# A gated memory-attention mixer and MLP on one core: two side units fewer in the third step, x requested ahead of weights, the last full output pass ahead of the last side units

## The chip, the core and the metric

The kernel runs on one core of a Trainium2 chip. The metric is the device time of one execution in microseconds (us). Engines are TensorE (PE, with its weight loads PEld), VectorE (DVE), ScalarE (ACT), GpSimd (POOL) and SyncE (SP), which here only issues DMAs. A line number such as L689 is a line of the kernel as it was before; where the changed kernel is meant, lines from L587 on stand two lower in the file (L689 is L691 there; those between L901 and L903 one lower).

## What is computed

Two branches over the same 2048 tokens of 512 channels, mixed by a gate per token. Branch A is an attention of 32 heads of 128 that goes through the tokens in 64 segments of 32, one after the other, since the first 8 rows of each segment's output are the memory of the next. Branch B is a layer norm and an MLP of width 1376.

```python
for s in range(n_seg):                       # 64 segments, a recurrence through mem
    xs = x[:, s * seg_len:(s + 1) * seg_len, :]
    h = jnp.concatenate([mem, xs], axis=1)   # 8 + 32 rows
    q = jnp.einsum('btd,dhe->bhte', h, Wq)   # k and v likewise
    scores = jnp.einsum('bhqe,bhke->bhqk', q, k) * scale
    scores = jnp.where(mask[None, None], scores, -1000000000.0)
    p = _softmax(scores, axis=-1)
    o = jnp.einsum('bhqk,bhke->bhqe', p, v)
    o = jnp.einsum('bhte,hed->btd', o, Wo)
    mem = o[:, :M, :]
    outs.append(o[:, M:, :])
b = _gelu(_layernorm(x) @ w1 + b1) @ w2 + b2
out = g * a + (1 - g) * b                    # g = sigmoid(x . gate_w)
```

## The kernel before

**The dense phase** (to about 68 us) is the MLP, in 8 blocks of two tiles of 128 tokens. A block has 11 chunks `fc` of the width: `a_mm` multiplies normed x by a chunk of w1, ACT applies the gelu, and two chunks later `b_mm` multiplies by w2. For nine of the sixteen tiles (`DEF`) the second product is put off: `spill` stores their gelu outputs to DRAM (`h_dr`). Between chunks, by a table of `fc` written out in the loop (L566 to L595), stand the preparation of the next block (`prep` on DVE at `fc` 0, with the statistics of x, L436, and normed y, L454; `prep_tr`, PE's transposes L461, at `fc` 8 and 9), the gate's dot products (`gate_sums`, L467), and the loads. `loads_x` requests two tiles of x; x has six buffers, and L467 is their last reader. `loads` requests two quarter-matrices of attention weights of 1 MB each, and in block 6 the four parts of Wo. All of these DMAs are issued by SP in the order of the program: an issue that has to wait holds up all that stand behind it. In block 6 `first_h` also prepares the first step (L512 on PE, L513 on DVE).

**The recurrence** is 64 steps `s`, four per tile `T` (`si` is the step within the tile). A step on PE: projections of q and k (L129), scores (L267, L271), v (L148), sums of exponents, value products (L291, L296), the output pass (`wo_pass`, L160, from UT), and three small products `new_mem` (L761) that make the next step's memory rows, which DVE casts into `hT` (L763); the next step's projections need them. The output pass takes UT, whose rows of the previous step POOL has normalized (`x_norm`, L745) with reciprocals that went to DRAM and back spread over partitions (`r_dr`, L730, then `Rb`, L733, both on SP).

Waits in a step are filled with other work. `fill` is a generator that `run(n)` advances, eight units in a step; `side` says what it does: projections of the 8 leftover tokens of each segment (`GL`) for the next tile, or their output pass (`wo_left`, from UL), or, where there is neither, units of the MLP that was put off. The third step (`s` = 2, `T` = 0, `si` = 2) has `mlp_units(8)`. One such unit is two halves (`next(mlp)`), and each half is four matmuls of 128x256 into bank W (L689). Beside that every step runs two or three halves of its own. A chunk `hm` comes from DRAM in a DMA of 32 KB; as many are requested in a step's middle (`recip_x`, L661, between r_dr and Rb on SP) as were used up since.

A tile has 11 chunks, 22 halves. When the last one is done, `mlp_out` has DVE scale bank W into `ct` (L673) and SP store it (L674). `mlp_outs`, which calls it, is called at the end of each step, and by the generator ahead of the first half on a new chunk:

```python
        while hms:
            T, fc, hm, n = hms.pop(0)
            mlp_outs()
            for h in range(2):
```

**The end.** The last step leaves the loop after its v projections. Then come the sums of its exponents (L278), the selection `out_sel` of tile T-1 (L230, L234), three units of `wo_left` for tile T, the full output pass of step 62 into bank W (`wo_pass`, called in L903), the reciprocal and the scaling of E on DVE (L901 to L906), the value products, five more units of `wo_left`, and the last output product.

Of the kernel before, what the change touches and what calls it, by code (L numbers as in the profile page):

```python
# [28 lines left out]
def kernel(ctx, tc, A_x, A_mem0, A_Wq, A_Wk, A_Wv, A_Wo, A_seg_len, B_x, B_w1, B_b1, B_w2, B_b2, gate_w, out):  # L29
# [83 lines left out]
    X1 = lps.tile([P, 512], FP32)  # L113
# [42 lines left out]
    def wo_group(bk, U_, n):  # L156
        j, ih = HORD[n]
        for c in range(4):
            i = 4 * ih + c
            nc.tensor.matmul(bk[32 * c:32 * c + 32, :], lhsT=U_[:, j, i, :], rhs=Wo_sb[:, 4 * i + j, :],  # L160
                             start=(n == 0), stop=(n == NW - 1), tile_position=(0, 32 * c))
# [13 lines left out]
    def left_qk(T, t, hf, bk):  # L175
        for kc in range(KC):
            qk_unit(bk, gl(T), t, hf, kc)
            if kc < KC - 1:
                yield
        def ca():  # L180
            Tb = qk_cast(bk[:])
            dve_q.append(lambda: qk_tr(Tb, QL[T % 2], hf) if t == 0 else kl_tr(Tb, T, hf))
        act_q.append(ca)
        yield
# [30 lines left out]
    def wo_left(T, bk):  # L215
        for n in range(NW):
            wo_group(bk, UL[T % 2], n)
            if n < NW - 1:
                yield

        def ca():
            wl = cw.tile([P, Dm], BF16, tag="wl", name="wl")
            nc.scalar.copy(out=wl[:], in_=bk[:])
            wls[T] = wl
        act_q.append(ca)
        yield
# [75 lines left out]
    with tc.tile_pool(name="mlpw", bufs=1) as mlpw, \  # L302
# [13 lines left out]
        def ld_x(T, eng=nc.sync):  # L316
            xt = mwork.tile([P, Dm], BF16, tag="xt", bufs=6, name="xt")
            eng.dma_start(xt[:], x2[T * P:(T + 1) * P, :])
            xts[T] = xt

        def ld_w(W_, A, n):
            nc.sync.dma_start(W_[:, n, :], A[n * P:(n + 1) * P].rearrange("p h e -> p (h e)"))

        def ld_o(i):
            nc.sync.dma_start(Wo_sb[:, i:i + 8, :], A_Wo[i:i + 8].rearrange("h e d -> e h d"))
# [28 lines left out]
        def loads_x(blk):  # L354
            if 2 * blk + 7 < NT:
                ld_x(2 * blk + 6)
                ld_x(2 * blk + 7)

        def loads(blk):
            if blk == 3:  # L360
                nc.sync.dma_start(m0[:], A_mem0[0])

            for kc in range(2 * blk, min(2 * blk + 2, 3 * KC)):
                ld_w(*((Wv_sb, A_Wv), (Wq_sb, A_Wq), (Wk_sb, A_Wk))[kc // KC], kc % KC)
            if blk == 6:
                for i in range(0, H, 8):
                    ld_o(i)
# [89 lines left out]
        def prep_tr(blk, tt):  # L457
            y, bk = ys.pop(blk * TB + tt), (X1, X2)[tt]
            tp = bk[:].bitcast(BF16)[:, 0:Dm].rearrange("p (k t) -> p k t", k=KC)
            for kc in range(KC):  # L460
                nc.tensor.transpose(tp[:, kc, :], y[:, kc * P:(kc + 1) * P], ident[:])  # L461
            nc.vector.tensor_copy(out=yTs[blk][:, :, tt * P:(tt + 1) * P], in_=tp)

        def gate_sums(blk):
            for T in range(blk * TB, blk * TB + TB):
                junk = mwork.tile([P, Dm], BF16, tag="junk", bufs=1, name="junk")
                nc.vector.scalar_tensor_tensor(out=junk[:], in0=xts.pop(T)[:], scalar=1.0, in1=gw_bc[:], op0=ALU.mult, op1=ALU.mult, accum_out=z_all[:, T:T + 1])  # L467

        def gates(blk):
            t0, t1 = blk * TB, blk * TB + TB  # L470
            nc.scalar.activation(out=th[:, t0:t1], in_=z_all[:, t0:t1], func=ACTF.Tanh, scale=0.5)
            if blk == NBLK - 1:
                nc.vector.tensor_scalar(out=g_all[:], in0=th[:], scalar1=0.5, scalar2=0.5, op0=ALU.mult, op1=ALU.add)
            nc.vector.tensor_scalar(out=omg[:, t0:t1], in0=th[:, t0:t1], scalar1=-0.5, scalar2=0.5, op0=ALU.mult, op1=ALU.add)
# [4 lines left out]
        def a_mm(blk, fc):  # L479
            rows = min(P, F - fc * P)  # L480
            n = blk * FC + fc
            hp = (SbF, W, U[1], U[3])[n % 4]
            for kc in range(KC):
                nc.tensor.matmul(hp[:rows, 0:TB * P], lhsT=w1_sb[:, kc, fc * P:fc * P + rows], rhs=yTs[blk][:, kc, :], start=(kc == 0), stop=(kc == KC - 1))  # L484
            nc.scalar.activation(out=hTm[blk % 2][:rows, :, fc, :], in_=hp[:rows, 0:TB * P].rearrange("p (t c) -> p t c", t=TB), func=ACTF.Gelu_apprx_tanh, bias=b1_sb[:rows, fc:fc + 1], scale=1.0)

        def b_mm(blk, fc):
            rows = min(P, F - fc * P + 1)
            tts = [tt for tt in range(TB) if blk * TB + tt not in DEF]
            for tt in tts:  # L490
                nc.tensor.matmul(bp(blk, tt)[:], lhsT=hTm[blk % 2][:rows, tt, fc, :],
                                 rhs=w2_sb[:rows, fc, :], start=(fc == 0), stop=(fc == FC - 1))
            if fc == FC - 1:
                for tt in tts:
                    ct_out(blk, tt)

        def spill(blk, a, b):
            for tt in range(TB):
                T = blk * TB + tt
                if T in DEF:  # L500
                    nc.sync.dma_start(h_dr[T][:, a:b], hTm[blk % 2][:, tt, a:b])
# [53 lines left out]
        for n, (blk, fc) in enumerate(units):  # L555
            a_mm(blk, fc)
            if n == len(units) - 1:
                dummy = msmall.tile([P, 1], FP32, tag="dummy", name="dummy")
                nc.scalar.activation(out=dummy[:], in_=omg[:, 0:1], func=ACTF.Exp)
            if n >= LAG:  # L560
                b_mm(*units[n - LAG])
            if fc == 0:
                if blk >= 1:
                    gates(blk - 1)
                if blk + 1 < NBLK:
                    prep(blk + 1)  # L566
                else:
                    gate_sums(blk)
                    for _ in consts():
                        pass  # L570
            if blk + 1 < NBLK:
                f0 = 8
                if fc == 7:
                    spill(blk, 0, 6)
                if fc == 2 and blk >= 1:
                    spill(blk - 1, 6, FC)
                if fc == 3 and blk >= 1:
                    loads_x(blk - 1)
                if fc in (f0, f0 + 1):
                    prep_tr(blk + 1, fc - f0)  # L580
                if fc == f0 + 1:
                    gate_sums(blk)
                if fc == 8:
                    loads(blk)
                if blk == NBLK - 2 and fc == 4:
                    first_h()
            elif fc >= 1:  # L587
                if fc == 2:
                    spill(blk - 1, 6, FC)
                if fc == 3:  # L590
                    gates(blk)
                if fc == 7:
                    spill(blk, 0, 6)
# [34 lines left out]
    def run(n):  # L628
        for _ in range(n):
            next(fill, None)  # L630
# [5 lines left out]
    def side(T, si):  # L636
        gens = []
        if si == 2:
            gens = [wo_left(T - 1, X1) if T >= 1 else mlp_units(8)]
        elif T + 1 == NT:  # L640
            gens = [mlp_units(4)] if si < 2 else []
        else:
            gens = [[left_qk(T + 1, 0, 0, X1), left_qk(T + 1, 1, 0, U[3])], [left_qk(T + 1, 0, 1, X1), left_qk(T + 1, 1, 1, U[3])], [],
                    [left_v(T + 1, 0, X1), left_v(T + 1, 1, U[3])]][si]
        return chain(*gens)
# [51 lines left out]
    def mlp_units(n):  # L697
        for _ in range(n):
            next(mlp, None)
            next(mlp, None)  # L700
            yield
# [45 lines left out]
    def wo_pass(U_, cuts=(0, Dm), bk=W):  # L747
        for n in range(NW):
            wo_group(bk, U_, n)
        w = cw.tile([P, Dm], BF16, tag="w", bufs=8, name="w")  # L750
        for a, b in zip(cuts, cuts[1:]):
            nc.scalar.copy(out=w[:, a:b], in_=bk[:, a:b])  # L752
        return w
# [14 lines left out]
    for s in range(nseg):  # L768
        T, si = divmod(s, SPT)
# [127 lines left out]
    for _ in out_sel(T - 1, X1):  # L897
        pass
    fill = wo_left(T, X2)
    run(3)  # L900
    nc.vector.reciprocal(out=R[:, nx], in_=SbF[:, 0:32 * NG])  # L901
    nc.scalar.activation(out=rmin[:, nx], in_=R[:, nx], func=ACTF.Copy, accum_out=tot[:, 3:4])
    ws[s - 1] = wo_pass(UT[s % 2])  # L903
    Rr = R[:, nx].rearrange("p (i q) -> p i q", q=32)
    nc.vector.tensor_tensor(out=E[:, :, 8:40], in0=E[:, :, 8:40], in1=Rr, op=ALU.mult)
    nc.vector.tensor_tensor(out=E[:, :, 0:8], in0=E[:, :, 0:8], in1=Rr[:, :, 0:8], op=ALU.mult)  # L906
# [176 lines left out]
```

## Time and profile before

| | us |
|---|---|
| median of 3 runs | 747.87 (745.25 to 749.37) |
| the profiled execution | 750.09 |
| its span, first to last instruction | 748.2 |
| PE busy | 732.8 |
| ACT busy | 536.7 |
| DVE busy | 448.9 |
| POOL busy | 246.6 |
| mean granted clock of TensorE | 0.997 |

The span is what the page and the trace divide up; the rest of the time lies around it. Most steps of the recurrence take 10.15 to 10.5 us from the first projection to the next step's; the third, fourth and fifth take 12.28, 12.73 and 12.06. A row of a timeline reads: start, duration from the first to the last of the merged instructions, engine, line, operation, output<-input, shapes, count, and in brackets the idle time before it with what ended it. A row of waits reads: engine, tile and line, what it waited for, the sum in us, how often, the longest. A row of windows has, after its bounds and length, the busy time and count of each engine, the granted clock, the DMA engines' busy share, and GB/s.

### The profile page before, as it was taken

To read this page: it belongs to the slowest core of one execution; us is meant where nothing else is said; L and a number is where in the kernel's file an instruction comes from. 1 tells how busy PE (TensorE), PEld (TensorE's weight loads), DVE (VectorE), ACT (ScalarE), POOL (GpSimd) and SP (SyncE) were. 2 spreads that over 40 slices of the span, in tenths; PEclk is the share of its full clock that TensorE was granted. 3 is DMA by queue.
4 is the path that set the end of the run, shared out by engine and by line. 5 is a ranking of instruction groups with operands and counts; after the bars stand their busy time and mean duration, and the time that the engine had idled before them with its cause. 6 is when DMAs were issued, how large, how long until landed. Compare 5 with 4: busy or idle time off the path is not lost. (4 is left out here: it accounts for less than half of the span.)

```text
span 748.2 us, 44010 instructions
## 1 busy us (share of the span) xinstructions
PE 732.8 (98%) x19147; PEld 428.8 (57%) x19147; DVE 448.9 (60%) x1541; ACT 536.7 (72%) x1629; POOL 246.6 (33%) x515
## 2 busy tenths in 40 slices
PE   8999998999999999999999999999999999999997
PEld 5776554556565555555555555555555555555553
DVE  6877554656565555656565665556665656555554
ACT  6777765777777777777777777777777777777664
POOL 4001332332334333343234334243333343333331
PEclk9999999999999999999999999999999999999999
DMA  8999222222222323122321323231322313222221
GB/s 308 343 360 360 84 83 55 69 87 80 78 68 62 97 74 93 47 83 80 93 79 38 96 75 97 69 81 57 92 78 82 85 44 94 69 90 70 85 63 61
DMA packets 61944, 76.82 MB, mean 103 GB/s; under 512 B 26729, under 2 KB 51922, under 8 KB 60210
## 3 DMA queue, kind: packets, MB, share of 16 engines
q1 hardware_dynamic: 60802, 72.51, 31.1%
q8 instruction: 151, 2.47, 1.3%
q0 software_dynamic: 400, 0.92, 0.3%
q10 hardware_dynamic: 544, 0.52, 0.2%
q14 instruction: 47, 0.39, 0.2%
HBM read 60.21 MB, written 7.70 MB: 91 GB/s over the span
## 5 line engine op out<-in xcount | busy, mean ns | idle before, releaser
L134 ACT CAST Tb<-U 128x512 bf16<-128x512 f32 x288 | 168.8, 586 | 82.5 <-PE U L129 76.8
L745 POOL TENSOR_TENSOR UT<-XR,Rb 128x384 bf16<-128x384 bf16 x126 | 114.1, 927 | 324.6 <-DMA Rb<-r_dr 228.0
L129 PEld LDWEIGHTS <-hT 128*32 128x32 bf16 x4096 | 108.8, 97 | 97.8 <-issue 2.0
L129 PE MATMUL U<-Wq_sb,hT 128*32 128x512 bf16 x2048 | 145.9, 382 | 0.4 <-DVE hT L763 0.4
L129 PE MATMUL U<-Wk_sb,hT 128*32 128x512 bf16 x2048 | 145.2, 381 | 0.0
L148 PE MATMUL X<-Wv_sb,hT 128*32 128x512 bf16 x2048 | 142.9, 378 | 0.0
L160 PE MATMUL X<-Wo_sb,UT 128*32 128x512 bf16 x2016 | 120.8, 380 | 0.0
L834 ACT CAST V<-X 128x256 bf16<-128x256 f32 x256 | 88.7, 372 | 16.0 <-PE X L148 1.1
L138 DVE STREAM_TRANSPOSE QT<-Tb 128x256 f32<-128x256 f32 x128 | 57.0, 445 | 71.1 <-ACT Tb L134 70.9
L763 DVE CAST hT<-U 128x8 bf16<-128x8 f32 x126 | 20.8, 167 | 130.9 <-PE U L761 96.6
L160 PEld LDWEIGHTS <-UT 128*32 128x32 bf16 x2048 | 56.4, 96 | 55.7 <-issue 16.6
L721 ACT CAST XR<-U 128x256 bf16<-128x256 f32 x252 | 78.6, 438 | 0.0
L752 ACT CAST w<-X 128x128 bf16<-128x128 f32 x189 | 44.8, 310 | 41.7 <-PE X L160 41.0
L138 DVE STREAM_TRANSPOSE KT<-Tb 128x256 f32<-128x256 f32 x128 | 57.0, 445 | 25.9 <-ACT Tb L134 25.9
L737 POOL TENSOR_TENSOR racc<-racc,R 128x128 f32<-128x128 f32 x63 | 28.8, 457 | 105.7 <-DVE R L735 101.1
L148 PEld LDWEIGHTS <-hT 128*32 128x32 bf16 x2048 | 45.2, 95 | 20.6
L689 PE MATMUL W<-w_sb,hm 128*32 128x256 bf16 x728 | 50.5, 273 | 3.6 <-DMA hm<-h_dr 3.6
L865 ACT CAST UT<-U 128x64 bf16<-128x64 f32 x252 | 35.4, 227 | 25.9 <-PE U L296 25.9
L745 POOL TENSOR_TENSOR UL<-XR,Rb 128x128 bf16<-128x128 bf16 x126 | 51.5, 430 | 0.0
L809 ACT ACTIVATE E<-U 128x64 bf16<-128x64 f32 (+1 forms) x128 | 35.0, 273 | 9.3 <-PE U L271 0.4
L484 PEld LDWEIGHTS <-w_sb 128*128 128x128 bf16 (+1 forms) x352 | 34.1, 100 | 10.4
L160 PE MATMUL X<-Wo_sb,UL 128*32 128x512 bf16 x512 | 38.7, 379 | 1.0 <-POOL UL L896 1.0
(184 smaller groups left out, 1250.5 us busy)
## 6 DMA issues: line engine op xcount, KB each, us to landing
Rb<-r_dr SPq DMA_DIRECT2D x63, 512.0 KB, 3.9
Wv_sb<-in_A_Wv_dram SPq DMA_DIRECT2D x4, 1024.0 KB, 7.5
Wq_sb<-in_A_Wq_dram SPq DMA_DIRECT2D x4, 1024.0 KB, 8.5
Wk_sb<-in_A_Wk_dram SPq DMA_DIRECT2D x4, 1024.0 KB, 8.4
Wo_sb<-in_A_Wo_dram SPq DMA_DIRECT2D x4, 1024.0 KB, 12.6
VP<-VL SPq DMA_DIRECT2D x64, 64.0 KB, 3.7
hm<-h_dr SPq DMA_DIRECT2D x91, 32.0 KB, 2.6
c<-c_dr SPq DMA_DIRECT2D x16, 128.0 KB, 4.6
```

Source lines behind the costliest of these rows:

```text
L129: nc.tensor.matmul(bk[32 * j:32 * j + 32, :], lhsT=G[:, kc, :], rhs=W5[t][:, kc, h0:h1, j, :], start=(kc == 0), stop=(kc == KC - 1), tile_ ...
L134: nc.scalar.copy(out=Tb[:], in_=bk.rearrange("p (a b e) -> p a e b", a=8, b=2))
L138: nc.vector.transpose(out=dst[:, 8 * hf:8 * hf + 8, c0:c0 + 32, :].rearrange("p a r b -> p a (r b)").bitcast(FP32), in_=Tb[:].rearrange("p ...
L148: nc.tensor.matmul(bk[32 * j:32 * j + 32, :], lhsT=G[:, kc, :], rhs=Wv5[:, kc, 4 * vb:4 * vb + 4, j, :], start=(kc == 0), stop=(kc == KC - ...
L160: nc.tensor.matmul(bk[32 * c:32 * c + 32, :], lhsT=U_[:, j, i, :], rhs=Wo_sb[:, 4 * i + j, :], start=(n == 0), stop=(n == NW - 1), tile_po ...
L689: nc.tensor.matmul(W[32 * c:32 * c + 32, cc], lhsT=hm[:, 32 * c:32 * c + 32], rhs=w2_sb[:, fc, cc], start=(fc == 0 and h == 0), stop=(fc = ...
L721: nc.scalar.copy(out=XR[:, j], in_=U[j][:, 0:NG * 40].rearrange("p (i q) -> p i q", q=40)[:, :, 0:32])
L745: nc.gpsimd.tensor_tensor(out=out[:, :, 4 * h:4 * h + 4, o:o + b - a], in0=XR[:, :, 4 * h:4 * h + 4, a:b], in1=Rb[:, h, :, :, r:r + b - a] ...
L752: nc.scalar.copy(out=w[:, a:b], in_=bk[:, a:b])
L809: nc.scalar.activation(out=E[:, 4 * i2:4 * i2 + 4, c], in_=Sb[i2][:, :, c], func=ACTF.Exp, scale=scale)
L834: nc.scalar.copy(out=V[:, i0:i0 + 2, :].rearrange("p i e -> p (i e)"), in_=(X1, X2)[vb][:, 256 * h:256 * h + 256])
L865: nc.scalar.copy(out=UT[s % 2][:, j, :, 0:M], in_=U[j][:, 0:NG * 40].rearrange("p (i q) -> p i q", q=40)[:, :, 32:40])
```

## The change

Three edits. The MLP side units of the third step are six instead of eight. In the dense phase, x is requested at `fc` 10 of its own block instead of `fc` 3 of the next, and the weights, from the second block on, right behind it at `fc` 10 instead of `fc` 8. After the loop, the last full output pass stands ahead of the three units of `wo_left`. No instruction is added or removed on any engine.

```diff
-                if fc == 3 and blk >= 1:
-                    loads_x(blk - 1)
...
-                if fc == 8:
+                if fc == 8 and blk == 0:
                     loads(blk)
+                if fc == 10:
+                    loads_x(blk)
+                    if blk:
+                        loads(blk)
...
         if si == 2:
-            gens = [wo_left(T - 1, X1) if T >= 1 else mlp_units(8)]
+            gens = [wo_left(T - 1, X1) if T >= 1 else mlp_units(6)]
...
     fill = wo_left(T, X2)
-    run(3)
     nc.vector.reciprocal(out=R[:, nx], in_=SbF[:, 0:32 * NG])
     nc.scalar.activation(out=rmin[:, nx], in_=R[:, nx], func=ACTF.Copy, accum_out=tot[:, 3:4])
     ws[s - 1] = wo_pass(UT[s % 2])
+    run(3)
```

The halves of the MLP form one sequence through the whole recurrence, so taking four out of the third step moves every later one: each stands two steps or so further on, up to the 63rd step, which now runs the last two.

On DVE, the first emptying of bank W stood before at the end of the third step, behind the casts of the new memory:

```order
L260 CAST SbF<-MkF 128x336
L763 CAST hT_86<-U_118 128x8
L763 CAST hT_86<-U_119 128x8
L763 CAST hT_86<-SbF 128x2x8
L673 TENSOR_SCALAR ct<-W,omg 128x512
L888 TENSOR_TENSOR rmin<-rmin,R 128x128
```

Now it (L675) stands in the middle of the fifth step, between the normalization of the memory rows' scores and the reciprocals of that step:

```order
L826 RECIPROCAL SbF<-SbF 128x32
L827 TENSOR_TENSOR E<-E,SbF 128x4x16
L826 RECIPROCAL RS<-U_121 128x32
L827 TENSOR_TENSOR E<-E,RS 128x4x16
L675 TENSOR_SCALAR ct<-W,omg 128x512
L728 TENSOR_REDUCE SbF<-SbF 128x2x8
L729 RECIPROCAL R<-SbF 128x64
```

The same move is made at the end of every eighth step after that, so that such an emptying now stands within the steps 5, 13, 21, 29, 37, 45, 53 and 61; the ninth and last is at the end of step 63 instead of step 62.

On PE at that place of the fifth step, the second half that the step runs of its own, behind leftover projections. In brackets is what an instruction waits for. Before:

```order
L129 MATMUL X_122<-Wq_sb,GL 32x512
L689 LDWEIGHTS hm [waits DMAHW4_49]
L689 MATMUL W<-w_sb,hm 32x256
L689 LDWEIGHTS hm
L689 MATMUL W<-w_sb,hm 32x256
```

Now it is the first half of a new tile, and its first matmul waits for DVE. This wait stands on PE eight times, and nowhere on a matmul of L689 before:

```order
L129 MATMUL X_122<-Wq_sb,GL 32x512
L691 LDWEIGHTS hm [waits DMAHW7_49]
L691 MATMUL W<-w_sb,hm 32x256 [waits DVE_49]
L691 LDWEIGHTS hm
L691 MATMUL W<-w_sb,hm 32x256
```

On SP, the DMAs of the second block of the dense phase and the first of the third. Before:

```order
L501 DMA h_dr_70<-hTm_145 128x768
L322 DMA Wv_sb<-in_A_Wv_dram 128x4096 x2
L501 DMA h_dr_70<-hTm_145 128x640
L318 DMA xt<-in_A_x_dram 128x512 x2
L501 DMA h_dr_71<-hTm_144 128x768
L322 DMA Wq_sb<-in_A_Wq_dram 128x4096 x2
```

Now:

```order
L501 DMA h_dr_70<-hTm_145 128x768
L318 DMA xt<-in_A_x_dram 128x512 x2
L322 DMA Wv_sb<-in_A_Wv_dram 128x4096 x2
L501 DMA h_dr_70<-hTm_145 128x640
L501 DMA h_dr_71<-hTm_144 128x768
L318 DMA xt<-in_A_x_dram 128x512 x2
```

Each pair of weights has moved behind a pair of x. In the last two blocks that load weights there is no x left to request, and their loads stand where they stood, right behind the block's first store.

## Prediction

> **What bounds the kernel now.** I read the page's busy times first, then the waits of PE in order of their sum, then the timeline of PE where those waits lie.
>
> ```profile
> span 748.2 us, 44010 instructions
> PE 732.8 (98%) x19147; PEld 428.8 (57%) x19147; DVE 448.9 (60%) x1541; ACT 536.7 (72%) x1629; POOL 246.6 (33%) x515
> PE W L689 <- DMA hm<-h_dr: 3.6, 3, 2.4
> ```
>
> PE is busy for 98% of the span, so whatever leaves PE waiting is paid in full, and work off PE is free until PE waits for it. The largest wait of PE on anything is the third row: three times, 3.6 us in all, 2.4 us at the longest, PE stood ready with a side unit (L689) whose chunk `hm` had not landed. The next view, by windows, shows what the longest one cost beside itself (columns: PE, PEld, DVE, ACT, POOL busy, granted clock, DMA share, GB/s).
>
> ```profile
> 116.00:118.00 2.00, 0.04 (x4) 0.04 (x8) 0.00 (x0) 0.37 (x1) 0.00 (x0) 1.00 0.21 42
> 118.00:120.00 2.00, 2.00 (x47) 0.99 (x51) 0.71 (x4) 0.58 (x1) 0.00 (x0) 0.75 0.81 247
> 120.00:122.00 2.00, 2.00 (x24) 0.84 (x20) 0.71 (x2) 0.58 (x1) 0.78 (x1) 0.50 0.28 86
> 122.00:124.00 2.00, 2.00 (x56) 1.03 (x52) 0.71 (x3) 1.17 (x2) 1.81 (x4) 0.89 0.29 66
> 250.00:252.00 2.00, 1.18 (x59) 0.73 (x55) 1.69 (x8) 1.22 (x6) 0.56 (x3) 1.00 0.00 0
> ```
>
> After the 2.4 us of idleness the granted clock was 0.75, 0.50 and 0.89 in three windows of 2 us: 0.50 + 1.00 + 0.22 = 1.72 us of PE work lost. The last row has 0.82 us of idleness at a clock that stayed 1.00: short waits did not do this.
>
> **The side units: what goes.** PE's timeline at the end of the third step, of the fourth, and of the 62nd, which before the change has no side work left:
>
> ```profile
> 101.53 1.91 PE L160 MATMUL X<-Wo_sb,UT 128*32 128x512 bf16 x32
> 103.26 0.73 PE L689 MATMUL W<-w_sb,c 128*32 128x256 bf16 x20
> 105.90 0.39 PE L129 MATMUL U<-Wq_sb,hT 128*32 128x512 bf16 x4
> ...
> 113.22 1.91 PE L160 MATMUL X<-Wo_sb,UT 128*32 128x512 bf16 x32
> 118.63 0.40 PE L129 MATMUL U<-Wq_sb,hT 128*32 128x512 bf16 x4
> ...
> 716.87 1.94 PE L160 MATMUL X<-Wo_sb,UT 128*32 128x512 bf16 x32
> 719.70 0.40 PE L129 MATMUL U<-Wq_sb,hT 128*32 128x512 bf16 x4
> ```
>
> The output pass takes PE 103.26 - 101.53 = 1.73 us. From its end to the next step's first projection the 62nd step needs 719.70 - 716.87 - 1.73 = 1.10 us with no side unit between: that is the chain of output cast, new-memory matmuls and their casts. The third step takes 105.90 - 103.26 = 2.64 us, because its last two units wait for chunks issued in that same step. They are the two units that the change drops there, so the step ends 2.64 - 1.10 = 1.54 us earlier. The fourth step takes 118.63 - 113.22 - 1.73 = 3.68 us; with four halves less behind it, the half that waited now needs a chunk loaded a step earlier, and 3.68 - 1.10 = 2.58 us go. Without that idleness the clock has no cause to fall: 1.72 us. **Together -5.84 us.** The dropped units are 16 matmuls, some 0.4 us of PE (209.01 to 209.11 below is 0.10 for a half); they come back in the 62nd and 63rd step, where one of four halves lies in a gap: +0.3 us.
>
> **The side units: what comes.** Units are counted in halves, and 22 halves fill bank W for one tile. Before, the count reaches 22, 44, ... at the end of a step, where DVE empties W (L673) while PE has five microseconds of projections before the next half. With four halves less at the start every count slips: the 22nd half is the first one of a step, the 23rd follows in the same step, and the order above shows PE's 23rd half waiting for DVE and L673 standing in the middle of DVE's step. This happens eight times. The same place of the 13th step, one of the eight, and the duration of L673:
>
> ```profile
> 208.20 0.28 PE L689 MATMUL W<-w_sb,hm 128*32 128x256 bf16 x4
> 208.58 0.60 PE L129 MATMUL X<-Wq_sb,GL 128*32 128x512 bf16 x8
> 209.01 0.28 PE L689 MATMUL W<-w_sb,hm 128*32 128x256 bf16 x4
> 209.11 0.19 PE L715 MATMUL SbF<-E,BO 128*32 128x40 bf16 x4
> 209.10 0.23 DVE L825 TENSOR_TENSOR E<-E,RS 128x64 bf16<-128x64 bf16 x1
> 106.73 0.75 DVE L673 TENSOR_SCALAR ct<-W,omg 128x512 bf16<-128x512 f32 x1 [0.40 <-issue]
> ```
>
> W is complete at 208.48, but DVE is in the normalization until 209.33; L673 then runs to about 210.05 (neighbours overlap by some 0.05). PE wanted its half at 209.01: a wait of 1.04 us, with the second half of the scores' sums, the value matmuls and the output pass queued behind it on PE, and the reciprocals behind L673 on DVE. Nothing later in such a step is idle on PE to take it back. Seven times 1.04 is 7.3; in the 61st step side units fill the place of the L129 row (0.43 to the next row), so the 23rd half comes that much earlier relative to DVE: 1.47. **Together +8.7 us.** The trace before has no such wait. Its bounds: 0 if W is emptied in time; 8 x (0.75 + 0.85) = 12.8 if each also waits for DVE's pair ahead of it at its full length (209.33 - 208.48 = 0.85). I keep 8.7, which goes by rows of the same place.
>
> On the clock the Trainium skill has two rules (TensorE: Matmul & The Clock Gate). The section on what is happening puts the drop after at least one idle window of about 3.4 us; here 2.4 us sufficed, so the trace decides, and by the page the 1.72 us would not go: the sum would be 1.7 higher. The section on PSUM-queue cycling says that frequent short idleness between matmul groups makes the clock oscillate: that speaks against this change and is a rival below.
>
> **x ahead of weights.** In the dense phase (to 68 us) DVE prepares a block two tiles at a time.
>
> ```profile
> 55.28 0.17 DVE L474 TENSOR_SCALAR omg<-th 128x2 f32<-128x2 f32 x1 [0.27 <-ACT th L471]
> 55.99 0.69 DVE L436 BATCH_NORM_STATS2 st<-xt 128x6 f32<-128x512 bf16 x1 [0.54 <-DMA xt<-in_A_x_dram]
> 60.42 0.17 DVE L513 COPY hT<-X 128x32 bf16<-128x32 bf16 x1
> 60.64 0.38 PE L461 MATMUL X<-ident,y 128*128 128x128 bf16 x4 [0.59 <-DVE hT L513]
> ```
>
> The last block's x lands 0.6 us late behind 2 MB of weights; L513, and with it PE's transposes, are as much later. With x first in the queue: **-0.6 us**. The cost is on SP, which issues in order.
>
> ```profile
> 43.26 1.26 SPq L322 DMA_DIRECT2D Wk_sb<-in_A_Wk_dram  x2
> 46.66 0.69 DVE L467 SCALAR_TENSOR_TENSOR junk<-xt,gw_bc 128x512 bf16<-128x512 bf16 x1
> 47.01 0.95 SPq L318 DMA_DIRECT2D xt<-in_A_x_dram  x2
> 40.00:60.00 20.00, 20.00 (x164) 14.78 (x162) 16.17 (x62) 14.99 (x35) 2.45 (x6) 1.00 0.99 368
> SPq L661 <- DMA Wo_sb<-in_A_Wo_dram: 3.2, 2, 2.9
> 78.19 1.82 SPq L103 DMA_TRANSPOSE xT<-in_A_x_dram  x1
> 80.17 0.56 SPq L730 DMA_DIRECT2D r_dr<-R  x1
> 86.98 1.81 POOL L745 TENSOR_TENSOR UT<-XR,Rb 128x384 bf16<-128x384 bf16 x2 [5.54 <-ACT Tb L134]
> 90.64 2.08 PE L160 MATMUL X<-Wo_sb,UT 128*32 128x512 bf16 x32
> ```
>
> x reuses a buffer that L467 reads last, so the second x cannot leave before 47.4; an issue takes some 0.5 (0.95 for two), and weights now stand behind it and leave at about 47.9 instead of 43.26, 4.6 us later, in four blocks. DMA is 99% busy here, so a hole is hardly made up. The first shift opens one of at most 4.6; x's own bytes (0.26 MB at 368 GB/s, 0.7) and 1 to 2% of slack over 50 us (0.6 to 1) fill part. I take 2.6 us for how much later Wo, the last weight, lands; bounds 0 and 4.6. SP's `hm` loads wait for Wo, and behind them stand xT and r_dr, with 0.1 us of air. r_dr leads through Rb to UT on POOL (its row names ACT, but what ACT makes for it is a step old; Rb is the late input), done at 88.79, which the second step's output pass needs at 90.64: 1.85 of slack, 1.22 when PE comes 0.63 earlier. So PE waits 2.6 - 0.1 - 1.2 = **+1.3 us** there (0 to 3.3).
>
> **The last output pass.** It goes ahead of three units that wait for POOL:
>
> ```profile
> 736.38 0.40 PE L234 MATMUL X<-wl,SelL 128*32 128x512 bf16 x4
> 737.74 0.83 PE L160 MATMUL X<-Wo_sb,UL 128*32 128x512 bf16 x12 [0.96 <-POOL UL L896]
> 740.23 0.27 PE L291 MATMUL U<-E,V 32*128 32x40 bf16 x16
> 734.87 1.80 POOL L745 TENSOR_TENSOR UT<-XR,Rb 128x384 bf16<-128x384 bf16 x2 [6.66 <-DMA Rb<-r_dr]
> 738.66 0.22 DVE L906 TENSOR_TENSOR E<-E,R 128x64 bf16<-128x64 bf16 x1
> ```
>
> UT is ready at 736.67, when PE is free at 736.6; 1.73 of pass and 0.66 of units end at 739.1, after E at 738.9. So the value matmuls start 740.23 - 739.1 = 1.1 us earlier and all behind them: **-1.1 us**. W's last emptying now comes one step before, with its store and reload of c; that has some 9 us until DVE uses c.
>
> **Sum.** -5.84 + 0.3 + 8.7 - 0.6 + 1.3 - 1.1 = +2.8 us. The profiled execution took 750.09 (748.2 of span, 1.9 around it) and would take 752.9; it is 2.2 above the median of the runs shown, 747.87, against which I forecast 747.87 + 2.8, **750.6 us**, 0.4% more. A measurement of this kernel (745.25 to 749.37) can tell about 0.5%, 3.7 us, from no change.
>
> **The rivals.** 1, the eviction is hidden: PE's new waits end early, and only 0.3 - 5.84 - 0.6 + 1.3 - 1.1 = -5.9 remains: 741.9. For it: DVE is 60% busy. Against: DVE's rows above put its normalization exactly there. Chance 0.12. 2, late weights, the slower end: Wo lands the full 4.6 us later and PE stands 3.3 us in the second step, longer than the 2.4 that lowered the clock, so another 1.72 goes: 750.6 + 2.0 + 1.72 = 754.3. It decides from a delay of about 3.7 on. For it: DMA at 99%. Against: the other queues' stores move into the hole. Chance 0.17. 3, each of the eight waits lowers the clock for as long as the one at 118: 8 x 1.72 on top, 764.4. Against: the 250 to 252 row. Chance 0.04. 4, the chunks are late all the same, and the 5.84 stay: 756.5; against it, the chunks are one step older. Chance 0.04. The forecast has 0.63.
>
> **How the numbers follow.** The forecast's own range, from waits of 0.85 to 1.2 us and a delay of Wo of 0 to 3.6, is 747 to 753.5; about a sixth of it lies above 751.6. Slower: 0.10 + 0.14 + 0.04 + 0.04 = 0.32. Faster: 0.11 from the first rival. Within 0.5%: 0.57. For 8 in 10 I reach to 745 below and 754.5 above, which leaves out most of rival 1, 3 and 4.
>
> **What would show it.** The wait of L689 on hm gone, and a clock of 1.00 from 118 to 124. In its place eight waits of PE at L691 on DVE, 1.0 us each. PE's transposes at L461 without a wait. UT later than PE in the second step, released by Rb. The value matmuls of the last step right behind the three units. Wrong would be: no wait on L675 above 0.5 us; a wait on Wo, VP or hm in the first steps over 2 us; granted clock below 1.00 in other places than the ends.

## The result, and the profile after

| | before | after |
|---|---|---|
| median of six runs, us | 746.82 (745.25 to 749.37) | 753.35 (752.18 to 755.94) |
| ratio, 95% interval | | 1.0088 (1.0062 to 1.0113) |
| profiled execution, us | 750.09 | 753.42 |
| its span, us | 748.2 | 751.6 |

The changed kernel is 0.9% slower: 6.5 us between the medians, but only 3.4 us between the two profiled spans. That difference is itself one of the results; first the page. Its head, and the view of waits cut to PE's waits that matter and to ACT's on `h_dr` (in us: total, times, longest):

```profile
span 751.6 us, 44018 instructions
PE 731.7 (97%) x19139; PEld 429.3 (57%) x19147; DVE 449.4 (60%) x1541; ACT 536.4 (71%) x1629; POOL 247.0 (33%) x515
PE W L691 <- DVE ct L675: 9.0, 8, 1.3
ACT hTm L485 <- DMA h_dr<-hTm: 3.7, 3, 2.1
...
PE U L491 <- ACT hTm L485: 1.2, 1, 1.2
PE X L461 <- ACT hTm L485: 0.7, 1, 0.7
```

PE has nearly the same work (731.7 us busy against 732.8, of which 1.7 was work stretched by the lower clock) in a span 3.4 us longer. The wait on `hm` is gone. In its place stand eight waits on DVE's emptying of W, 9.0 us, as forecast, and two in the dense phase that were not forecast: PE behind the gelu, and the gelu behind the store of `h_dr`. Next, the windows of the place where the clock fell before (columns as in the prediction):

```profile
116.00:118.00 2.00, 2.00 (x48) 0.87 (x38) 0.47 (x3) 1.32 (x3) 0.00 (x0) 1.00 0.66 237
118.00:120.00 2.00, 2.00 (x60) 1.09 (x56) 1.59 (x4) 1.40 (x3) 0.00 (x0) 1.00 0.55 150
...
122.00:124.00 2.00, 0.68 (x20) 0.22 (x8) 1.44 (x3) 0.65 (x2) 0.71 (x2) 1.00 0.00 0
```

The clock column (third from the end) is 1.00 throughout, and PE is full until 122 (one window like these is left out). The idleness of 1.32 us in the last row is the first of the eight waits, and it left the clock alone. Now PE and DVE at the same place as in the prediction, the 13th step, first PE and then DVE:

```profile
205.00 0.29 PE L691 MATMUL W<-w_sb,hm 128*32 128x256 bf16 x4
...
206.84 0.29 PE L691 MATMUL W<-w_sb,hm 128*32 128x256 bf16 x4 [0.85 <-DVE ct L675]
```

```profile
205.45 0.35 DVE L826 RECIPROCAL RS<-U 128x32 f32<-128x32 f32 x1
205.90 0.23 DVE L827 TENSOR_TENSOR E<-E,RS 128x64 bf16<-128x64 bf16 x1
206.04 0.74 DVE L675 TENSOR_SCALAR ct<-W,omg 128x512 bf16<-128x512 f32 x1
```

W is complete at 205.29, DVE comes to it at 206.04 after the second half of the normalization, and PE gets its 23rd half at 206.84. To say what each stretch of the program gained or lost, the first projection of a step on PE serves as a clock; these are the starts of the 1st, 3rd, 6th, 13th, 62nd and 64th step, of before and then of after:

```profile
72.93 0.39 PE L129 MATMUL U<-Wq_sb,hT 128*32 128x512 bf16 x4
93.62 0.40 PE L129 MATMUL U<-Wq_sb,hT 128*32 128x512 bf16 x4
130.69 0.39 PE L129 MATMUL U<-Wq_sb,hT 128*32 128x512 bf16 x4
202.82 0.40 PE L129 MATMUL U<-Wq_sb,hT 128*32 128x512 bf16 x4
709.54 0.40 PE L129 MATMUL U<-Wq_sb,hT 128*32 128x512 bf16 x4
730.09 0.39 PE L129 MATMUL U<-Wq_sb,hT 128*32 128x512 bf16 x4
```

```profile
74.42 0.39 PE L129 MATMUL U<-Wq_sb,hT 128*32 128x512 bf16 x4
94.94 0.40 PE L129 MATMUL U<-Wq_sb,hT 128*32 128x512 bf16 x4
127.93 0.39 PE L129 MATMUL U<-Wq_sb,hT 128*32 128x512 bf16 x4
199.62 0.40 PE L129 MATMUL U<-Wq_sb,hT 128*32 128x512 bf16 x4
713.73 0.40 PE L129 MATMUL U<-Wq_sb,hT 128*32 128x512 bf16 x4
734.65 0.39 PE L129 MATMUL U<-Wq_sb,hT 128*32 128x512 bf16 x4
```

Subtracting neighbours, and the last start from the span, gives this table (us, after minus before):

| stretch | forecast | measured |
|---|---|---|
| dense phase | -0.6 | +1.49 |
| 1st and 2nd step | +1.3 | -0.17 |
| 3rd to 5th step (the first of the eight waits is in the 5th) | -5.84 + 1.04 = -4.8 | -4.08 |
| 6th to 12th step | 0 | -0.44 |
| 13th to 61st step (seven waits) | +7.7 | +7.39 |
| 62nd and 63rd step | +0.3 | +0.37 |
| last step and end | -1.1 | -1.16 |
| **sum** | **+2.8** | **+3.4** |

Between the two profiled executions the sum was off by 0.6 us, in part by luck: the dense phase came out 2.1 us worse than forecast and the first two steps 1.5 us better. Three questions remain: why the medians differ by 6.5, what the dense phase lost, and whether the eight waits are the loss they seem to be.

### The profile page after: what moved, and what is told of

Its sections match the earlier page's. It is cut to its first block, busy times and chain, and to the rows that moved or that the text cites. A ratio compares the mean times of both kernels' runs of the same rounds, so it can differ in the third digit from the quotient of the medians.

```text
span 751.6 us, 44018 instructions
## 1 busy us (share of the span) xinstructions
PE 731.7 (97%) x19139; PEld 429.3 (57%) x19147; DVE 449.4 (60%) x1541; ACT 536.4 (71%) x1629; POOL 247.0 (33%) x515
## 4 chain that ended last, share of the span: by engine, by line
PE 89%; DVE 4%; DMA 4%; ACT 1%; issue 1%; SPq 1%; DVEq 0%; POOL 0%; ACTq 0%; POOLq 0%
PE U L129 33%; PE X L160 19%; PE X L148 15%; PE X L129 3%; PE U L291 3%; PE W L691 3%; DMA h_dr<-hTm 2%; PE U L148 2%; DMA Wq_sb<-in_A_Wq_dram 1%; PE U L267 1%; PE U L484 1%; PE U L491 1%; DVE E L827 1%; PE SbF L267 1%; DVE ct L675 1%
## 5 line engine op out<-in xcount | busy, mean ns | idle before, releaser
L129 PE MATMUL U<-Wk_sb,GL 128*32 128x512 bf16 x496 | 39.3, 377 | 0.0
## 6 DMA issues: line engine op xcount, KB each, us to landing
Wo_sb<-in_A_Wo_dram SPq DMA_DIRECT2D x4, 1024.0 KB, 11.7
```

Of the source, the lines that this page charges most:

```text
L129: nc.tensor.matmul(bk[32 * j:32 * j + 32, :], lhsT=G[:, kc, :], rhs=W5[t][:, kc, h0:h1, j, :], start=(kc == 0), stop=(kc == KC - 1), tile_ ...
```

## Experiments

Every time below stands against runs of the kernel before on the same chip; a ratio is given with its 95% interval.

### The three edits one at a time

**Six side units alone:**

```diff
-            gens = [wo_left(T - 1, X1) if T >= 1 else mlp_units(8)]
+            gens = [wo_left(T - 1, X1) if T >= 1 else mlp_units(6)]
```

> The kernel before with six side units in the third step, and nothing else of the change. Theory A (the eight mid-step emptyings of bank W are the loss): the third and fourth step get 1.5 to 2.6 us shorter each and the half-clock stretch at 118 us goes, together -5.8; PE waits eight times for DVE at the 23rd half, 1.0 to 1.3 us each and 8.7 to 9.0 in all; sum +3 us against before, and the first step starts at 72.9 us as before. Theory B (the loss of the change comes from the order of the loads, and the emptyings are made up elsewhere): -5.5 us. If the measured +6.5 us of the whole change were all from the units: +6.5.

Measured: 753.49 us, ratio 1.0065 (1.0045 to 1.0086), +4.9 us. PE waits eight times for DVE at the 23rd half, 8.3 us in all; the first step starts at 72.44. Theory A's waits are there, and the loss of the change is here for the most part; it is somewhat larger than the +3 forecast, for the reason that a later run gives.

**The order of the loads alone:**

```diff
-                if fc == 3 and blk >= 1:
-                    loads_x(blk - 1)
...
-                if fc == 8:
+                if fc == 8 and blk == 0:
                     loads(blk)
+                if fc == 10:
+                    loads_x(blk)
+                    if blk:
+                        loads(blk)
```

> The kernel before with x requested ahead of the weights at the end of a block, and nothing else of the change. Theory A (the spills of the gelu's output now stand in the queue behind 2 MB of weights, the gelu waits for them, PE for the gelu): ACT waits three times for h_dr at L485, 3 to 4 us in all, PE about 1.9 us in the dense phase, the first step starts 1.5 us later than before's 72.93; the second step has its old length; total +1.5 us. Theory B (the prediction's): the dense phase is 0.6 us shorter and PE waits 1.3 us in the second step for UT, +0.7 us. With the chunk loads of the third and fourth step later too, either may be larger: the waits of L689 on hm would then be over the 3.6 us of before.

Measured: 749.94 us, ratio 1.0018 (0.9996 to 1.0041), +1.4 us, not told from nothing. And its one profiled execution, the fastest of its twelve (745.23 us), went against theory A: ACT waited once for `h_dr`, 0.5 us, PE never for the gelu, and the first step started at 72.31, 0.6 earlier than before. It was as theory B had it in the dense phase, while the same instructions had lost 1.49 us there in the changed kernel. So what the order costs differs from one execution to the next, and more executions of it were needed (below).

**The last pass alone:**

```diff
-    run(3)
     nc.vector.reciprocal(out=R[:, nx], in_=SbF[:, 0:32 * NG])
     nc.scalar.activation(out=rmin[:, nx], in_=R[:, nx], func=ACTF.Copy, accum_out=tot[:, 3:4])
     ws[s - 1] = wo_pass(UT[s % 2])
+    run(3)
```

> The kernel before with the last full output projection ahead of the last three side units, and nothing else. The prediction's term: -1.1 us, all of it after 736 us, by the value matmuls of the last step starting 1.1 us earlier. Rival: the end is set by another chain (the last tile's c, or DVE's tail) and nothing is gained: 0.

Measured: 747.33 us, ratio 0.9989 (0.9965 to 1.0012): too small to be told from nothing by the time. The trace shows it. PE's timeline of the end of this kernel:

```profile
734.00 0.29 PE L278 MATMUL SbF<-E,BO 128*32 128x256 bf16 x4 [0.17 <-ACT E L809]
...
737.06 0.27 PE L291 MATMUL U<-E,V 32*128 32x40 bf16 x16
```

From the sums (L278) to the value matmuls (L291) it is 3.06 us, with the output pass between them and no wait; in the first profile of before it was 4.21, from 736.02 to 740.23, with 0.96 of waiting. Against that profile the gain is 1.15 us, as forecast. In the second profile of before (below) the same stretch is 3.89 us, from 733.63 to 737.52, with 0.65 of waiting: against that one it is 0.83.

The three edits alone add up to 4.9 + 1.4 - 1.2 = 5.1 us, where the whole change measured 6.5; intervals of 1.5 to 2 us to either side leave that open.

### Where W is emptied

Six units shift the count of halves by four. One more half in the fourth step brings the 22nd half back to the end of a step.

```diff
-            gens = [wo_left(T - 1, X1) if T >= 1 else mlp_units(8)]
+            gens = [wo_left(T - 1, X1) if T >= 1 else mlp_units(6)]
...
         if si:
             next(mlp, None)
+        if s == 3:
+            next(mlp, None)
```

> Six units in the third step and one more half in the fourth, so that the 22nd half of each tile is again the last of a step; nothing else of the change. Theory A (the place of W's emptying is the loss): the eight waits of PE on DVE at the 23rd half go, the gain of the third and fourth step stays: -5.5 us against before, some 8.5 us below the kernel with six units alone. Rival (moved halves themselves cost, not the emptying): within 1 us of the kernel with six units alone, +3 us.

Measured: 744.06 us, ratio 0.9940 (0.9923 to 0.9958), -4.5 us, and 9.4 us below the kernel with six units alone, which ran beside it. No wait on `ct` is left. One half in another place decides the sign of the change.

The other way to take the wait away is to leave the count as it is and to let DVE empty W ahead of the second half of the normalization, on top of the six units:

```diff
             if s:
                 next(mlp, None)
+                mlp_outs()
             msum(1)
```

> Six units alone, but DVE empties W right behind the 22nd half, ahead of the second half of the normalization. Theory A (the wait is DVE's order: W is complete 0.85 us before DVE comes to it): PE's eight waits at the 23rd half fall from 1.0 to 1.3 us each to 0 to 0.4, but the normalization is 0.75 us later, and the sums and value matmuls behind it, so 0 to 0.75 of the 1.0 comes back as a wait on E or on the sums: 0 to 6 us below the kernel with six units alone, best guess 3. Rival (the bank hand-over itself costs): the waits stay at 1 us.

Measured: 748.60 us, ratio 1.0021 (1.0001 to 1.0041), +1.6 us: 0.44% or 3.3 us below the kernel with six units alone, by the two ratios. The view of waits of PE and DVE's timeline in the 13th step:

```profile
PE W L689 <- DVE ct L673: 3.0, 8, 0.7
```

```profile
202.38 0.22 DVE L825 TENSOR_TENSOR E<-E,SbF 128x64 bf16<-128x64 bf16 x1
202.52 0.74 DVE L673 TENSOR_SCALAR ct<-W,omg 128x512 bf16<-128x512 f32 x1
...
203.63 0.23 DVE L825 TENSOR_TENSOR E<-E,RS 128x64 bf16<-128x64 bf16 x1
```

The order of two DVE instructions took the eight waits from 8.3 to 3.0 us. In the 13th step DVE now begins L673 0.16 us after W is complete (202.36 and 202.52) instead of 0.75, and PE still waits 0.27 us there, for L673 itself; the longest of the eight, 0.7, lies outside the 0 to 0.4 of theory A. The normalization ends 0.7 us later, and part of the gain goes back through it, as theory A said. Most of the wait was DVE's order, then; a bank whose hand-over itself cost 1 us would have kept it.

### The kernel before, a second time

> The kernel before, unchanged, profiled a second time. Theory A (the profiled execution of before, 750.09 us, was one with late chunks, and the 5.8 us that six units take off were read from it too large): the third to fifth step, 37.1 us together in the first profile, take 33 to 35 us, with no window under clock 1.00 near 118 us or a shorter one; span 745 to 746 us. Rival (the stall is the same each time): 36.5 to 37.5 us, clock 0.5 to 0.75 near 118 us. Time: ratio 1.000 either way.

Measured: 746.23 us, ratio 0.9995 (0.9976 to 1.0014), span 745.5. The windows around its late chunk:

```profile
114.00:116.00 2.00, 0.52 (x12) 0.03 (x4) 0.00 (x0) 1.20 (x4) 0.21 (x2) 1.00 0.19 41
116.00:118.00 2.00, 1.69 (x48) 0.98 (x52) 0.71 (x4) 0.59 (x1) 0.00 (x0) 1.00 0.47 166
118.00:120.00 2.00, 2.00 (x44) 0.96 (x36) 1.09 (x3) 1.37 (x3) 0.00 (x0) 1.00 0.61 193
```

The late chunk left PE idle for 1.79 us instead of 2.40, and the clock stayed at 1.00. The third to fifth step took 33.75 us (starts at 93.70 and 127.45) where the first profile had 130.69 - 93.62 = 37.07. That is 3.3 us between two executions of one kernel, from a race between DMAs and PE, and as much as lies between the profiled 750.09 us and the median of six, 746.82. Theory A holds. Two more traces have eight units in the third step: with the load order alone these three steps took 33.99 us, with the last pass alone 33.38, and the late chunk left PE idle for 2.16 and 1.32 us at a clock of 1.00. The first profile is the one that stands apart.

How often does the clock fall? Each run's record has its mean granted clock. Of the 14 traces of all kernels, two have windows of 2 us under 1.00 (the first profile of before, and the kernel with a third gelu buffer below), and their means are 0.997 and 0.998; the twelve others have 0.999 or 1.000. Of the 95 runs of before that stood beside the experiments, 35 have 0.998 or less, with a median of 748.75 us, and 60 have 0.999 or more, with a median of 746.29. Of the 62 runs of the six kernels with six units and weights that leave as early as before, none has 0.998 or less. So the lowered clock that the prediction took off is in about one execution of before in three. Within each of the three sets of runs those executions are 1.7 to 2.2 us longer at the median (2.5 over all sets together, whose levels differ); the waits before the fall are part of that.

### Load order, more executions, and the better kernel

Two kernels with W emptied at the end of a step and the last pass ahead, first with the loads as before and then with x ahead:

> Six units and one more half in the fourth step (so that W is emptied at the end of a step) together with the last output projection ahead; order of the loads as before. If the pieces add up: -4.5 (measured for the first alone) - 0.8 to -1.1 = -5.3 to -5.6 us against before, 743 us. If the end is hidden: -4.5.

> The kernel of the run with W emptied at the end of a step and the last projection ahead, with x ahead of the weights as well: the whole change but for where W is emptied. Theory A (the order of the loads costs in most executions, by spills that the gelu waits for): 1 to 1.5 us above the kernel without it, ACT's waits at L485 on h_dr 2 to 4 us in all, first step at 73.5 to 74.5 us. Theory B (no cost, a gain of 0.6): 0.6 us below it, first step at 72.3. Against the changed kernel either is some 9 us lower.

Measured beside each other: 742.03 us, ratio 0.9937 (0.9913 to 0.9960), with the old order, and 744.43 us, ratio 0.9970 (0.9949 to 0.9991), with x ahead. The same two kernels again in another set of runs:

> W emptied at the end of a step and the last projection ahead, loads in the old order: a second run beside the others of this call. First step at 72.4 to 73.0 us, no wait on h_dr in the dense phase; time 742 us, ratio 0.994.

> The same with x ahead of the weights, a second run. Theory A (the late spills): 1 to 2.5 us above the kernel with the old order, ACT waiting 2 to 4 us for h_dr. Theory B (the first comparison was chance): equal within 0.7 us.

Measured: 741.77 us, ratio 0.9946 (0.9927 to 0.9965), and 744.91 us, ratio 0.9987 (0.9972 to 1.0001). The new order costs 2.4 and 3.1 us. What the last pass adds to the time cannot be told: the two runs with it and the old order are 5.0 and 4.5 us below before, the one without it was 4.5 below.

Where does the new order lose? In the chain of waits of the changed kernel (the page's chain, in order of time: start, us, what) the dense phase has this piece:

```profile
30.93 0.71 DVE junk L467 x2
...
31.66 0.33 SPq L318
...
32.05 0.42 SPq L322
...
32.52 10.70 DMA Wq_sb<-in_A_Wq_dram
...
43.29 9.47 DMA h_dr<-hTm
...
52.86 0.48 ACT hTm L485
...
53.39 0.39 PE U L491
```

Read downwards: x's request waits for L467, its buffer's last reader; the weights behind it on SP leave after it; the spill of the gelu's output is issued at 43.29, released by the landing of a weight load that was issued 11 us before it, and takes 9.47 us to land among weights; and the gelu that writes the same buffer two blocks later waits for it, and PE for the gelu. SP's waits in the dense phase, of before and then of after, show it at the queue:

```profile
SPq L318 <- DVE junk L467: 1.4, 4, 0.4
```

```profile
SPq L318 <- DVE junk L467: 16.1, 10, 3.4
...
SPq L501 <- DMA Wq_sb<-in_A_Wq_dram: 4.8, 2, 2.9
```

SP stood 16.1 us with x's requests, ten times, instead of 1.4, and 4.8 us with a spill behind a weight load. The second kind of wait is in the kernel before too, once, with 1.6 us, and in the kernel with the load order alone it is no longer than that (1.5); the long waits for L467 are in every trace with the new order (16.1 to 17.2). To test it by taking the wait's reason away, the gelu's output got a third buffer, on the kernel with the new order:

```diff
-        hTm = [mout.tile([P, TB, FC, P], BF16, name=f"hTm{i}") for i in range(2)]
+        hTm = [mout.tile([P, TB, FC, P], BF16, name=f"hTm{i}") for i in range(3)]
...
-            ct = mout.tile([P, Dm], BF16, tag="ct", bufs=3, name="ct")
+            ct = mout.tile([P, Dm], BF16, tag="ct", bufs=2, name="ct")
```

> W emptied at the end of a step, last projection ahead, x ahead of the weights, and a third buffer for the gelu's output (the c buffers of the dense phase go from three to two to make room). Theory A (with x ahead, the spill of a block is queued behind 2 MB of weights and the gelu two blocks later waits for its buffer): with a third buffer ACT's waits at L485 on h_dr are gone, PE loses the 1.2 us it stood at L491, the first step starts at 72.3 to 72.6 us, time 1 to 1.3 us below the same kernel with two buffers. Rival (the dense phase with this order is slower by DMA bandwidth or by chance): still 73.5 to 74.5.

Measured: 745.17 us, ratio 0.9992 (0.9973 to 1.0011), against 744.91 with two buffers in the same set. The dense phase did what theory A says: no wait of ACT on `h_dr`, first step at 72.45. But nothing was gained. PE's timeline of the first step of this kernel, and its windows:

```profile
78.75 0.27 PE L291 MATMUL U<-E,V 32*128 32x40 bf16 x16
81.17 0.21 PE L296 MATMUL U<-E,VP 32*128 32x64 bf16 x4 [2.14 <-DMA VP<-VL]
...
82.30 3.09 PE L160 MATMUL X<-Wo_sb,UT 128*32 128x512 bf16 x32
```

```profile
80.00:82.00 2.00, 0.83 (x32) 0.48 (x36) 0.34 (x1) 0.43 (x5) 0.94 (x3) 0.82 0.32 81
82.00:84.00 2.00, 2.00 (x24) 0.69 (x20) 0.00 (x0) 1.23 (x6) 0.00 (x0) 0.50 0.33 76
84.00:86.00 2.00, 1.80 (x32) 0.68 (x28) 0.00 (x0) 0.51 (x3) 0.00 (x0) 0.82 0.00 0
```

The weights are still late, and `VP`, the values of the leftover tokens, which SP sends right behind Wo and the last spills, is now what PE waits for: 2.14 us, and after it the output pass takes 3.09 us instead of 1.91 at a clock of 0.82, 0.50 and 0.82. This execution took 748.34 us, 3.2 above the median of its twelve, so not every one has the fall of the clock; why the median gained nothing is thereby only in part shown. The second run of the two-buffer kernel, whose dense phase lost little, had the same wait with 1.4 us:

```profile
PE U L296 <- DMA VP<-VL: 1.4, 1, 1.4
```

So the lateness was paid in the dense phase (through the gelu's buffer) in two traces and mostly in the first step (through VP) in two others; the kernel with the load order alone paid little in either (0.5 us of each wait), and one trace with the old order waited 0.6 us for VP too. The start of the second step counts both. With the old order it is 83.32 and 83.40 (before, twice), 82.83, 84.00, 82.76, 82.81, 83.64 and 83.03: median 83.2. With x ahead it is 84.81, 83.18, 84.25 and 84.67: median 84.5, and 86.57 with three buffers. **By these medians the new order costs 1.3 us there**, though the two groups overlap. The rest of the 2.4 and 3.1 us lies behind the second step at no one place. From the second to the last step a profiled execution with the old order took 638.8 and 639.4 us, and one with x ahead 642.8 and 641.1; but the kernel with W emptied at the end of a step, which has the old order, took 643.3. This part stays open.

The last variant asks for the forecast's own -0.6 us by itself. Eight buffers let x go ahead of the same block's weights without waiting for L467:

```diff
-            xt = mwork.tile([P, Dm], BF16, tag="xt", bufs=6, name="xt")
+            xt = mwork.tile([P, Dm], BF16, tag="xt", bufs=8, name="xt")
...
-                if fc == 3 and blk >= 1:
-                    loads_x(blk - 1)
...
                 if fc == 8:
+                    loads_x(blk)
                     loads(blk)
```

> W emptied at the end of a step and the last projection ahead; x is requested ahead of the weights of the same block, but from eight buffers instead of six, so that its request waits for no reader and the weights leave as early as before. The prediction's -0.6 us by itself: PE's 0.6 us wait at L461 for DVE's hT, which stands behind the last block's statistics and x, goes; no wait on h_dr over 0.5 us; first step at 72.0 us; time 0.6 us below the kernel with the old order. Rival (hT is late by something other than x): the 0.6 us stays.

Measured: 742.93 us, ratio 0.9958 (0.9940 to 0.9976), against 741.77 without it. DVE's statistics and PE's transposes of the last block:

```profile
55.19 0.69 DVE L436 BATCH_NORM_STATS2 st<-xt 128x6 f32<-128x512 bf16 x1
...
60.06 0.17 DVE L513 COPY hT<-X 128x32 bf16<-128x32 bf16 x1
```

```profile
60.28 0.38 PE L461 MATMUL X<-ident,y 128*128 128x128 bf16 x4 [0.40 <-DVE hT L513]
```

x is there in time (L436 waits for nothing), and PE still waits 0.40 of the 0.59 us. Nor was the other 0.2 x's. In the first run of the same kernel with the old order, x happened to be in time as well, and PE waited the full 0.59:

```profile
55.20 0.69 DVE L436 BATCH_NORM_STATS2 st<-xt 128x6 f32<-128x512 bf16 x1
60.32 0.38 PE L461 MATMUL X<-ident,y 128*128 128x128 bf16 x4 [0.59 <-DVE hT L513]
```

The transposes start 0.04 us apart in the two (60.32 and 60.28); with eight buffers PE only came to them 0.16 us later. DVE's own work between L474 and L513 sets the time. The rival holds, and the kernel is not faster: 742.93 against 741.77 us, with intervals that overlap.

## Why the prediction was right, and where it was wrong

It forecast 750.6 us; 753.35 came out, inside the range and near its upper end. That the eight waits outweigh the gain was right. That the whole stays within 0.5% was wrong: it is slower by 0.9%.

- **The eight waits on W: right, place and size.** 8.7 us forecast, 9.0 waited in the changed kernel, 8.3 with the units alone; taking them out by one half in another step is worth 9.4 us of time. The first rival (the eviction is hidden) and the third (each wait lowers the clock) are out: the waits are there, and the windows behind each of the eight have a clock of 1.00.
- **The stalls removed: right for the execution that was read.** The fourth step came 1.1 us after the third step's output pass (102.44 + 1.73 = 104.17, and the next projection at 105.27), as forecast, and the clock no longer fell. The fourth rival, chunks late all the same, is out.
- **The step that failed is the carrying of the sum to the median.** The profiled execution "is 2.2 above the median of the runs shown, 747.87, against which I forecast 747.87 + 2.8", the prediction says. That execution was long because of the very stall that the change removes: 3.3 us longer in those three steps than the kernel's second profile, by a wait that was longer and a clock that falls in one execution of three. What only some executions have cannot be subtracted from a median that does not have it. The sum itself gave 752.9 for the profiled execution, and the changed kernel's took 753.42; the median of six with the gain cut by those 3.3 us, 746.82 + 2.8 + 3.3, is 752.9 as well.
- **The order of the loads: right that weights are late, wrong in what waits for it.** The last part of Wo landed at 78.2 us instead of 76.2 (issued at 66.5 and 63.1, 11.7 and 13.1 us to landing), 2.0 us later where 2.6 was forecast. But the prediction sent the lateness to Rb and UT in the second step (+1.3), where PE lost nothing (10.14 us against 10.30). Two earlier users of the same queue were overlooked: the spill, which holds the gelu's buffer, and VP. Forecast +0.7 with x's gain; 2.4 and 3.1 us measured with the rest in place, of which 1.3 was traced; by itself, 1.4 us that cannot be told from nothing. That the sum for the profiled execution still came within 0.6 us is luck in this part: a term that did not come (+1.3) stood in for one that was left out (+1.49).
- **x's own gain: not there.** The forecast read PE's 0.59 us at L461 as the lateness of x; with x in time PE waits there all the same, and the transposes start 0.04 us earlier at most.
- **The last pass: right in its mechanism**, 1.1 forecast, 1.15 and 1.16 against the first profile of before, 0.83 against the second: a wait that was read from one execution here too.
- **The second rival** (Wo 4.6 us later and the clock falling in the second step) did not come in the profiled execution of the changed kernel. Its mechanism, a transfer late behind Wo and then a halved clock, did come with a third gelu buffer, in the first step and through VP, where 4 of 12 runs have a mean clock of 0.998 or less. Of the six runs of the changed kernel one has, 0.996, and it is the longest, 755.94 us.

The kernel with W emptied at the end of a step, the last pass ahead and the loads in their old order beats both: 742.03 and 741.77 us, 0.6% and 0.5% below the one before and some 11 us below the change. Its 15 runs lie between 740.65 and 743.11, the 61 of before in the same sets between 742.23 and 750.59: the late chunks, whose price differs by execution, are gone, as far as the clock and the traces show it.

## What to carry to other kernels

Before a stall is put into a sum as a gain, ask whether every execution has it: a wait for a DMA differs between executions, and its gain must be taken from the execution in which it was read, not from the median. When a count of work items shifts, find where the counter's events (a bank being emptied, a buffer turning over) now fall in the consumer's step; here half a unit more or less was worth 9 us. When a request is moved ahead in a queue, list everything behind it up to the first user that has no slack, the stores too, since a store holds the buffer it reads.

## What the runs showed of the hardware

**The clock fell after waits of some 2 us, and length alone does not decide.** A wait of 1.8 us (before, second profile) left the clock at 1.00; waits of 2.41 (before, first profile) and 2.14 us (three gelu buffers) lowered it; and one of 2.16 us, on a chunk at 116.27 us in the kernel with the load order alone, did not:

```profile
114.00:116.00 2.00, 0.11 (x4) 0.00 (x0) 0.00 (x0) 0.92 (x3) 0.00 (x0) 1.00 0.16 33
116.00:118.00 2.00, 1.73 (x48) 0.98 (x52) 0.71 (x4) 0.59 (x1) 0.00 (x0) 1.00 0.58 145
118.00:120.00 2.00, 2.00 (x44) 0.99 (x40) 1.13 (x3) 1.41 (x3) 0.10 (x1) 1.00 0.66 215
```

When it fell, the loss was the same both times, 1.72 us over three windows of 2 us (0.50 + 1.00 + 0.22, and 0.36 + 1.00 + 0.36). The Trainium skill (TensorE: Matmul & The Clock Gate, What's actually happening) says that activity is counted in a window of about 3.4 us that runs freely, so the phase matters: that two waits of one length end differently agrees with it. Its rule that a whole window of idleness must pass does not agree with a fall after 2.14 us.

**Eight short waits a run did not lower it.** 9.0 us in pieces of 0.85 to 1.32 us went by at 1.00. The Trainium skill (TensorE: Matmul & The Clock Gate, A second HAM failure mode: psum-queue depth-cycling) names frequent short idleness between groups of matmuls as a cause of an unsteady clock; eight waits some 82 us apart (eight steps), as here, did not make it so.

**A DMA's issue can wait for an unrelated DMA to land**: the row `SPq L501 <- DMA Wq_sb` has 4.8 us in two waits, of a store that shares no data with the load. In the trace of the changed kernel the store issued at 43.29 waits for the semaphore that the load of 32.52 sets as it lands, at 43.22; the store then uses that same semaphore for its own landing.
